# Four later pairs of attention on quarter arrays, one q copy on ScalarE, one multiplication on GpSimd

## The chip, the cores and the metric

The kernel runs on one core of one Trainium2 chip. The metric is the time of one execution on the device in microseconds; the median of three executions of the kernel before is 878.07 us (877.82 to 878.16). Engines are called as in the profile: PE is TensorE (PEld its weight loads), DVE is VectorE, ACT is ScalarE, POOL is GpSimd, SP is SyncE, and a "q" behind a name means the sequencer of that engine.

## The reference

Attention in chunks of 64 positions, head by head, and then a feed-forward layer with a squared ReLU on all 4608 tokens. All inputs are float32 but the two weights, which reach the kernel as 64-bit numbers (pairs of 32-bit words).

```
q_c, k_c, v_c = (t.reshape(8, 8, 9, 64, 64) for t in (q, k, v))   # batch, head, chunk, position, head_dim
scores = q_c @ k_c.T / 8
attn = exp(scores - max(scores))
attn = attn / (sum(attn) + 1e-9)
x = (attn @ v_c) as [4608 tokens, 512]
h = x @ w_in                       # 512 -> 2048
out = relu(h)**2 @ w_out           # 2048 -> 512
```

## The kernel before

**Tiling.** A pair is 128 tokens (two chunks of 64, all eight heads). There are 36 pairs in nine blocks of four. The code counts pairs from 0: pair u = 0 to 3 (the lead, block 0), u = 4 to 7 (block 1, "pairs five to eight"), and 8 to 35, which the class Quad handles. Per block the feed-forward layer has 16 steps; a step of block b and slice f multiplies x of 512 tokens by 128 columns of w_in (line 525, 12 matmuls of 512 columns into the bank h), squares the ReLU on ACT and DVE (lines 536 to 552), and two steps later multiplies by the 128 rows of w_out (line 562, 12 matmuls into four banks o). Each float32 factor is split into a high part and a low part (gh and gl, xh and xl), hence three matmuls for each product.

**Weights.** The 32 weight slices (16 of w_in, 16 of w_out) are converted on the chip before first use, by `convert_w` (line 138): on ACT two reads of the raw words (lines 148, 149), on DVE clamp, shift, sign and up (lines 154, 160, 166, 173), on ACT the high part (line 178), on DVE the low part (line 187, tiles wi and wo). Staging tiles `a` for this come in ABUFS = 3 buffers, used in turn. Slices are converted in the order i0, i1, o0, i2, o1, i3 and so on, while block 0 already runs; all of it is done when block 0 is.

**Attention of pairs 0 to 7 (class Pair).** q and k of a pair are turned by four PE transposes each (line 411). The turned q is copied into the tile qbd by `keep_q` (line 422) in two copies of 64 partitions, each into its own half of a tile whose other half is zero, so that one matmul can contract over 128 partitions; pairs 0 and 1 copy on DVE, the others on ACT. k is copied by ACT (line 426). `scores` is 16 matmul calls against the zero-padded q, 32 matmuls in the trace (line 434). Then on DVE the maximum (line 441) and the subtraction (line 445), on ACT the exponential (line 450), on DVE the sum (line 454), the addition of 1e-9 (line 457; on POOL for pairs 4 to 7), the reciprocal (line 460) and the multiplication (line 461). The result is turned by PE (line 472), copied by ACT (line 477), and multiplied by v (line 486, again 32 matmuls against a zero-padded tile vbd). ACT and DVE write the result as xh and xl (lines 497, 499). The intermediate results of pairs 4 to 7 go in turn through the two PSUM banks of the tile `both`.

**Quad (pairs 8 to 35).** Here scores and values run on quarters of the array (lines 289 and 333): matmuls with 64 contraction rows and 64 columns, four of them on different quarters, with results in the halves of the two banks of `both`; there is no zero padding.

**Order.** The class Plan writes the order of each engine's instructions by hand: every step is added with an engine, an assumed cost, what it reads and writes, and a rank; a simulated run in assumed times sorts them. On the device each engine takes its instructions strictly in that order and waits where something is not ready. The matmuls of the feed-forward layer keep their order among themselves (line="ffn"). Attention of pairs 4 to 7 ranks with the weight slices among which it is added (one pair for every four slices); the steps of pair 8 and later rank behind all conversions.

Of the kernel before, what the change touches and what calls it, by code (L numbers as in the profile page):

```python
# [10 lines left out]
F32 = mybir.dt.float32  # L11
# [4 lines left out]
ALU = mybir.AluOpType  # L16
AX = mybir.AxisListType
# [3 lines left out]
def kernel(  # L21
# [20 lines left out]
    nc = tc.nc  # L42
    B, H, S, D = q.shape
    NT, DM = out.shape
    DFF = w_in.shape[1] // 2
    P = 128
    CH = 64
    NCH = S // CH
# [6 lines left out]
    EXP_MIN = 2.0 ** -15  # L55
    EXP_MAX = 122879.9921875

    ABUFS = 3
    blocks = [4] * 9
    LAG = 2  # L60
    GBUFS = 2
# [43 lines left out]
    def slot_of(pair):  # L105
        return pair if pair < blocks[0] else pair % 2
# [88 lines left out]
    xt = {}  # L195
# [47 lines left out]
    def load_lead_v(pair):  # L243


        for c in range(2):
            bb, n0 = divmod(2 * pair + c, NCH)
            for h2, r in enumerate(halves):
                s = v[bb, h2:H:2, n0 * CH:(n0 + 1) * CH, :]
                nc.sync.dma_start(  # L250
                    out=vbd[slot_of(pair)][r, :, c, h2, :], in_=s.rearrange("h i d -> i h d")
                )
# [13 lines left out]
    class Quad:  # L266
# [26 lines left out]
        def top(self):  # L293
            self.m = att.tile([P, 2, HH, 1], F32, name=f"m{self.pair}", tag="nm", bufs=2)
            nc.vector.tensor_reduce(self.m, four[:, :, 0], axis=AX.X, op=ALU.max)  # L295

        def less(self):
            self.e = late["pool"].tile([P, HH, 2, CH], F32, name=f"e{self.pair}", tag="e")
            nc.vector.tensor_tensor(  # L299
                self.e.rearrange("p h c j -> p c h j"), four[:, :, 0], self.m.broadcast_to([P, 2, HH, CH]),  # L300
                op=ALU.subtract,
            )
# [10 lines left out]
        def norm(self):  # L313
            nc.vector.tensor_tensor(self.e, self.e, self.z.broadcast_to([P, HH, 2, CH]), op=ALU.mult)  # L314
# [66 lines left out]
    class Pair:  # L381
# [36 lines left out]
        def keep_q(self, s):  # L418
            r = halves[s]

            copy = nc.vector.tensor_copy if self.u < 2 else nc.scalar.copy
            copy(qbd[self.u % 2][r, :, s], self.psq[r])

        def keep_k(self):
# [31 lines left out]
        def small(self):  # L456
            (nc.vector if self.lead else nc.gpsimd).tensor_scalar_add(self.z, self.z, 1e-9)

        def norm(self):
            nc.vector.reciprocal(self.z, self.z)  # L460
            nc.vector.tensor_tensor(
                self.e, self.e, self.z.broadcast_to([P, H, CH]), op=ALU.mult
            )

# [26 lines left out]
        def place(self, part):  # L491
            b = block_of[self.u]
            j = self.u - first_pair[b]
            ps = self.xt.rearrange("p a c i -> p a (c i)")
            xh, xl = (x[:, :, j * P:(j + 1) * P] for x in x_of(b))
            if part == 0:
                nc.scalar.copy(xh, ps)
            else:
                nc.vector.tensor_tensor(xl, ps, xh.bitcast(F32), op=ALU.subtract)


    steps = [(b, f) for b in range(len(blocks)) for f in range(NF)]
# [101 lines left out]
    class Plan:  # L604
# [21 lines left out]
        def add(self, engine, cost, fn, reads=(), writes=(), size=0, line=None, slack=0.0, gate=None, side=0):  # L626


            n = len(self.ops)
            before = set()  # L630
            for t in reads:
                if t in self.writer:
                    before.add(self.writer[t])
            for t in writes:
                before.update(self.readers.get(t, ()))
                if t in self.writer:
                    before.add(self.writer[t])
            for t in writes:
                self.writer[t] = n
                self.readers[t] = set()  # L640
            for t in reads:
                self.readers.setdefault(t, set()).add(n)
            after = set() if gate is None else {gate}
            if line is not None:
                if line in self.last:
                    after.add(self.last[line])
                self.last[line] = n
            before.discard(n)
            if side:
                self.sides[n] = side  # L650
            self.ops.append((engine, cost, fn, before, after, size, self.rank, slack))
            return n
# [84 lines left out]
    def program():  # L737
# [2 lines left out]
        p = Plan()  # L740
        lead = blocks[0]
        add = p.add
        prs = [Pair(u) for u in range(NN)]

        def prepare():
            make_identity(nc, ident)
# [21 lines left out]
                    line="sp" if e == SP else None)  # L768

        def load_values(u):  # L770
            add(SP, 4 * ISSUE, lambda: load_lead_v(u), writes=[("v", slot_of(u))], size=P * DM * 4, line="sp")

        def x_names(pair, part):
            b = block_of[pair]
# [9 lines left out]
        def attention(u):  # L784
            x = prs[u]
            i = u % 2
            if x.lead:
                bq, bk, bs = ("o", 2 * i), ("o", 2 * i + 1), ("h", i)
            else:
                bq, bk, bs = (("at", next(turn_at) % 2) for _ in range(3))  # L790
            if 2 <= u < lead:
                bp, bx = bk, bq
            else:
                bp, bx = (("at", next(turn_at) % 2) for _ in range(2))
            x.banks = {"q": bq, "k": bk, "sc": bs, "pt": bp, "xt": bx}
            r = ["early"]
            wait = 0.0 if x.lead else SLACK
            add(PE, 4 * 0.11, lambda: x.turn(0), [("q", u), "ident"], [bq], slack=wait)
            for s in range(2):
                e = DVE if u < 2 else ACT  # L800
                add(e, ONE, lambda s=s: x.keep_q(s), [bq] + r, [("qbd", i, s)])
            add(PE, 4 * 0.11, lambda: x.turn(1), [("k", u), "ident"], [bk], slack=wait)
            add(ACT, ONE, x.keep_k, [bk] + r, [("raw", "qk"[i])])
            if u in (0, lead - 1):
                filler(x, "sc", bs, [bq, bk])
            add(PE, 1.05, x.scores, [("qbd", i, 0), ("qbd", i, 1), ("raw", "qk"[i])] + r, [bs],
                slack=wait)
            add(DVE, TWO, x.top, [bs], [("m", i)])
            add(DVE, TWO, x.less, [bs, ("m", i)] + r, [("e", i)])
            add(ACT, ONE, x.exps, r, [("e", i)])  # L810
            add(DVE, TWO, x.sums, [("e", i)] + r, [("z", i)])
            add(DVE if x.lead else POOL, 0.2 if x.lead else 0.41, x.small, [], [("z", i)])
            add(DVE, TWO + 0.2, x.norm, [("z", i)] + r, [("e", i)])
            if u in (0, lead - 1):
                filler(x, "pt", bp, [bs])
            add(PE, 4 * 0.11, x.turn_p, [("e", i), "ident"] + r, [bp], slack=wait)
            add(ACT, ONE, x.keep_p, [bp] + r, ["tt"])
            if u in (0, lead - 2, lead - 1):
                filler(x, "xt", bx, [bp])
            add(PE, 1.05, x.values, [("v", slot_of(u)), "tt"] + r, [bx], slack=wait)  # L820
            xh, xl = x_names(u, "h"), x_names(u, "l")
            add(ACT, ONE, lambda: x.place(0), [bx], xh)
            add(DVE, TWO, lambda: x.place(1), [bx] + xh, xl)

        def convert(n):
            words, clamp, shift, sign, up, high, low = convert_w(n)
# [198 lines left out]
```

## Time and profile before

| what | value |
|---|---|
| median of three executions | 878.07 us |
| the profiled execution itself | 878.62 us |
| span in its profile, first to last instruction | 876.8 us |
| outside of the span | 1.82 us |
| PE busy | 868.4 us, 99% |
| DVE busy | 443.3 us, 51% |
| ACT busy | 313.8 us, 36% |
| POOL busy | 8.5 us, 1% |

The rows below come from this one profiled execution. A row of the timeline has the start in us from the start of the span, the duration, the engine, the line, the operation, the tiles written and read, the shape and the number of merged instructions; in brackets stands the idle time of the engine before it and what ended that. Consecutive instructions of one engine overlap a little, so that a step takes less of an engine's order than its own duration: the distance from one start to the next tells what it takes.

### The profile page before, as it was taken

Reading aid. Unit: us, or ns where it says so; the run is one execution under the profiler, and the core shown is the slowest. Engines: PE = TensorE matmul, PEld = TensorE weight load, DVE = VectorE, ACT = ScalarE, POOL = GpSimd, SP = SyncE. Lnnn points to the kernel's source line nnn. Section 1 sums busy time; section 2 is a strip of 40 time slices with the busy share of each in tenths; the row PEclk is TensorE's granted clock in tenths of the full one; section 3 lists DMA queues with packets and bytes.
Section 4 is the critical chain, followed back from the end, with each engine's and each line's share of the span. In section 5 each row is a group of like instructions: output and inputs, shape, how many; then the busy total and the mean of one; then the engine's idle time right before and its main releaser. Section 6 shows DMA issues by size and latency. Waiting matters only on the chain.

```text
span 876.8 us, 15293 instructions
## 1 busy us (share of the span) xinstructions
PE 868.4 (99%) x5950; PEld 709.9 (81%) x5950; DVE 443.3 (51%) x770; ACT 313.8 (36%) x537; POOL 8.5 (1%) x16
## 2 busy tenths in 40 slices
PE   9999999999999999999999999999999999999998
PEld 7777778888888888888888888888888888888886
DVE  5999994333444445444544444445444544423222
ACT  5898874333322222222322232223222322222221
POOL 2000000000000000000000000000000000000000
PEclk9999999999999999999999999999999999999999
DMA  8896523233343223222322242224222241001001
GB/s 189 248 257 185 193 33 95 52 53 54 53 96 53 44 48 93 48 45 47 93 48 46 44 94 48 47 47 96 50 48 46 45 95 23 13 1 49 1 0 49
DMA packets 256856, 62.91 MB, mean 72 GB/s; under 512 B 241808, under 2 KB 250256, under 8 KB 256784
## 3 DMA queue, kind: packets, MB, share of 16 engines
q1 hardware_dynamic: 254528, 61.28, 31.3%
q8 instruction: 47, 0.77, 0.4%
q10 hardware_dynamic: 2256, 0.66, 0.3%
q14 instruction: 25, 0.20, 0.1%
HBM read 45.09 MB, written 9.44 MB: 62 GB/s over the span
## 4 chain that ended last, share of the span: by engine, by line
PE 82%; SPq 3%; issue 3%; DVE 1%; DMA 0%; ACT 0%; POOLq 0%; POOL 0%; DVEq 0%; ACTq 0%
PE h L525 40%; PE o L562 39%; PE both L333 2%; SPq L232 2%; PE both L289 1%; SPq L328 1%; SPq L263 0%; DMA k_raw<-in_k_dram 0%; DVE gl L552 0%; DMA v_raw<-in_v_dram 0%; DVE kt L281 0%; DVE wi L187 0%; DVE z L309 0%; PE both L486 0%; DVE e L314 0%
## 5 line engine op out<-in xcount | busy, mean ns | idle before, releaser
L525 PE MATMUL h<-xh,wi 128*128 128x512 f32 x1152 | 388.2, 394 | 1.4 <-ACT wi L178 1.0
L562 PE MATMUL o<-wo,gh 128*128 128x512 f32 x1152 | 355.9, 390 | 0.0
L525 PEld LDWEIGHTS h<-xh,wi 128*128 128x128 f32 x1152 | 215.7, 188 | 51.1 <-DVE wi L187 2.7
L562 PEld LDWEIGHTS o<-wo,gh 128*128 128x128 f32 x1152 | 215.4, 188 | 44.5
L562 PE MATMUL o<-wo,gl 128*128 128x512 f32 x576 | 224.2, 389 | 0.0
L525 PE MATMUL h<-xl,wi 128*128 128x512 f32 x576 | 223.9, 390 | 0.0
L552 DVE TENSOR_TENSOR gl<-g,gh 128x512 fp32r<-128x512 f32 x144 | 98.3, 683 | 186.5 <-ACT gh L549 186.5
L536 ACT ACTIVATE g<-h 128x512 f32<-128x512 f32 x144 | 85.5, 594 | 229.4 <-PE h L525 215.9
L549 ACT CAST gh<-g 128x512 fp32r<-128x512 f32 x144 | 89.6, 622 | 207.4 <-PE o L562 168.3
L540 DVE TENSOR_TENSOR g<-g 128x512 f32<-128x512 f32 x112 | 76.3, 681 | 169.1 <-ACT g L536 169.1
L562 PEld LDWEIGHTS o<-wo,gl 128*128 128x128 f32 x576 | 108.1, 188 | 22.6
L525 PEld LDWEIGHTS h<-xl,wi 128*128 128x128 f32 x576 | 108.2, 188 | 21.3
L295 DVE TENSOR_REDUCE m<-both 128x8 f32<-128x512 f32 x28 | 19.4, 691 | 39.6 <-ACT xh L345 39.6
L305 ACT ACTIVATE e<-e 128x512 f32<-128x512 f32 x28 | 17.7, 633 | 52.2 <-DVE e L299 52.2
L345 ACT CAST xh<-both 128x512 fp32r<-128x512 f32 x28 | 16.4, 587 | 37.0 <-PE both L289 36.0
L333 PEld LDWEIGHTS both<-p,v_raw 64*64 64x64 f32 x896 | 15.6, 134 | 9.9 <-issue 9.5
L281 DVE STREAM_TRANSPOSE kt<-k_raw 128x512 f32<-128x512 f32 x28 | 19.0, 678 | 8.1 <-DMA v_raw<-in_v_dram 4.2
L542 ACT ACTIVATE g<-g 128x512 f32<-128x512 f32 x32 | 20.2, 632 | 0.6
L318 DVE STREAM_TRANSPOSE et<-e 128x512 f32<-128x512 f32 x28 | 19.9, 712 | 1.0
L281 DVE STREAM_TRANSPOSE qt<-q_raw 128x512 f32<-128x512 f32 x28 | 19.6, 702 | 0.0
L347 DVE TENSOR_TENSOR xl<-both,xh 128x512 fp32r<-128x512 f32 x28 | 19.1, 681 | 0.8 <-ACT xh L345 0.8
L333 PE MATMUL both<-p,v_raw 64*64 64x64 f32 x896 | 19.4, 224 | 0.0
(84 smaller groups left out, 433.6 us busy)
## 6 DMA issues: line engine op xcount, KB each, us to landing
wiraw<-in_moe_w_in_dram SPq DMA_DIRECT2D x16, 512.0 KB, 6.1
woraw<-in_moe_w_out_dram SPq DMA_DIRECT2D x16, 512.0 KB, 6.2
out_dram<-ob SPq DMA_DIRECT2D x32, 256.0 KB, 2.5
q_raw<-in_q_dram SPq DMA_DIRECT2D x224, 32.0 KB, 2.2
k_raw<-in_k_dram SPq DMA_DIRECT2D x224, 32.0 KB, 2.2
v_raw<-in_v_dram SPq DMA_DIRECT2D x224, 32.0 KB, 2.2
p<-et SPq DMA_DIRECT2D x224, 32.0 KB, 1.9
vbd<-in_v_dram SPq DMA_DIRECT2D x32, 64.0 KB, 2.7
```

Source lines behind the costliest of these rows:

```text
L281: nc.vector.transpose(t.rearrange("p h i -> p (h i)"), pairs[self.pair][nm].rearrange("p h a d -> p (h a d)"))
L295: nc.vector.tensor_reduce(self.m, four[:, :, 0], axis=AX.X, op=ALU.max)
L318: nc.vector.transpose(self.et.rearrange("p h c n i -> p (h c n i)"), self.e.rearrange("p h c j -> p (h c j)"))
L333: nc.tensor.matmul(four[to, b, 1, 2 * a + c], self.v[own, c, a, t], self.p[own, 2 * a + t, c].rearrange("p n i -> p (n i)"), start=True, s ...
L347: nc.vector.tensor_tensor(xl, got, xh.bitcast(F32), op=ALU.subtract)
L525: nc.tensor.matmul(self.h[:, :self.n], a[:, c], bb[:, c, :self.n], start=c == 0 and i == 0, stop=last,)
L536: nc.scalar.activation(self.g, self.h[:, :self.n], AF.Relu)
L540: nc.vector.tensor_tensor(self.g, self.g, self.g, op=ALU.mult)
L542: nc.scalar.activation(self.g, self.g, AF.Square)
L549: nc.scalar.copy(self.gh[:, :self.n], self.g)
L552: nc.vector.tensor_tensor(self.gl[:, :self.n], self.g, self.gh.bitcast(F32)[:, :self.n], op=ALU.subtract)
L562: nc.tensor.matmul(acc[b, j], a[:, j * P:(j + 1) * P], bb, start=f == 0 and i == 0, stop=f == NF - 1 and i == 2,)
```

## The change

Five edits go together. Pairs 4 to 7 become a new class Later, which runs scores and values on quarters of the array, as Quad does: 16 calls each with 64 contraction rows, 32 matmuls in a trace, results in halves of both banks of `both`; q is kept without zero padding in one copy of 128 partitions on ACT; v is loaded by two DMAs in place of four. The two banks of `both` are then held in a fixed way (q and the turned probabilities in the first, k in the second, scores and values in halves of both). For these four pairs the multiplication of the probabilities by the reciprocal moves from DVE to POOL; the reciprocal itself stays on DVE as a step of its own (`part`). In the lead, q of pair 1 is copied by ACT and no longer by DVE. The staging tiles `a` get a fourth buffer. The plan's assumed costs follow: 0.6 in place of 1.05 us for scores and values, 1.1 us for the multiplication on POOL.

```diff
-    ABUFS = 3
+    ABUFS = 4
...
-            copy = nc.vector.tensor_copy if self.u < 2 else nc.scalar.copy
+            copy = nc.scalar.copy if self.u else nc.vector.tensor_copy
...
+        def part(self):
+            nc.vector.reciprocal(self.z, self.z)
+
         def norm(self):
-            nc.vector.reciprocal(self.z, self.z)
-            nc.vector.tensor_tensor(
+            (nc.vector if self.lead else nc.gpsimd).tensor_tensor(
...
+    class Later(Pair):
+        def half(self, n):
+            return four[:, :, n]
+        def load_values(self):
+            self.v = vbd[slot_of(self.u)][:, :HH // 2].rearrange("p a b c d -> p (a b c) d")
+            for c, r in enumerate(halves):
+                bb, n0 = divmod(2 * self.u + c, NCH)
+                s = v[bb, :, n0 * CH:(n0 + 1) * CH, :]
+                nc.sync.dma_start(out=self.v[r], in_=s.rearrange("h i d -> i h d"))
+        def keep_q(self):
+            self.qt = qbd[self.u % 2][:, :HS]
+            nc.scalar.copy(self.qt.rearrange("p h c i -> p (h c) i"), self.psq)
+        def scores(self):
+            out = self.half(0)
+            kt = self.kt.rearrange("p (h c) j -> p h c j", c=2)
+            for g, c, s, w in itertools.product(range(2), repeat=4):
+                own, to = halves[s], halves[w]
+                nc.tensor.matmul(
+                    out[to, s, 2 * g + c], self.qt[own, 2 * g + w, c], kt[own, 2 * g + w, c], start=True, stop=True
+                )
+        def top(self):
+            self.m = att.tile([P, H, 1], F32, name=f"nm{self.u}", tag="nm", bufs=2)
+            nc.vector.tensor_reduce(
+                self.m.rearrange("p (s h) a -> p s h a", s=2), self.half(0), axis=AX.X, op=ALU.max
+            )
+        def less(self):
+            self.e = nat.tile([P, H, CH], F32, name=f"ne{self.u}", tag=f"ne{self.u % 2}")
+            nc.vector.tensor_tensor(
+                self.e.rearrange("p (s h) j -> p s h j", s=2), self.half(0),
+                self.m.rearrange("p (s h) a -> p s h a", s=2).broadcast_to([P, 2, HH, CH]), op=ALU.subtract,
+            )
+        def turn_p(self):
+            self.pt = self.room("pt")
+            for a in range(HH):
+                nc.tensor.transpose(
+                    self.pt[:, a // 2, a % 2].rearrange("p s i -> p (s i)"),
+                    self.e[:, 2 * a:2 * a + 2].rearrange("p c j -> p (c j)"), ident,
+                )
+        def values(self):
+            out = self.half(1)
+            for a, w, c in itertools.product(range(HH), range(2), range(2)):
+                own, to = halves[c], halves[w]
+                nc.tensor.matmul(
+                    out[to, c, a], self.v[own, 2 * a + w], self.t[own, a // 2, a % 2, w], start=True, stop=True
+                )
+        def place(self, part):
+            b = block_of[self.u]
+            j = self.u - first_pair[b]
+            xh, xl = (
+                x[:, :, j * P:(j + 1) * P].rearrange("p h (c i) -> p c h i", c=2) for x in x_of(b)
+            )
+            if part == 0:
+                nc.scalar.copy(xh, self.half(1))
+            else:
+                nc.vector.tensor_tensor(xl, self.half(1), xh.bitcast(F32), op=ALU.subtract)
...
-        prs = [Pair(u) for u in range(NN)]
+        prs = [(Pair if u < lead else Later)(u) for u in range(NN)]
...
+            fn = (lambda: load_lead_v(u)) if u < lead else prs[u].load_values
+            add(SP, (4 if u < lead else 2) * ISSUE, fn, writes=[("v", slot_of(u))], size=P * DM * 4, line="sp")
...
-                bq, bk, bs = (("at", next(turn_at) % 2) for _ in range(3))
-            if 2 <= u < lead:
+                bq, bk = bs, bx = [("at", n) for n in range(2)]
+            if not x.lead:
+                bp = bq
+            elif u >= 2:
                 bp, bx = bk, bq
             else:
                 bp, bx = (("at", next(turn_at) % 2) for _ in range(2))
             x.banks = {"q": bq, "k": bk, "sc": bs, "pt": bp, "xt": bx}
             r = ["early"]
+            both_at = [("at", n) for n in range(2)]
+            sc, xt = ([bs], [bx]) if x.lead else (both_at, both_at)
             wait = 0.0 if x.lead else SLACK
             add(PE, 4 * 0.11, lambda: x.turn(0), [("q", u), "ident"], [bq], slack=wait)
-            for s in range(2):
-                e = DVE if u < 2 else ACT
-                add(e, ONE, lambda s=s: x.keep_q(s), [bq] + r, [("qbd", i, s)])
+            if x.lead:
+                for s in range(2):
+                    e = ACT if u else DVE
+                    add(e, ONE, lambda s=s: x.keep_q(s), [bq] + r, [("qbd", i, s)])
+            else:
+                add(ACT, ONE, x.keep_q, [bq] + r, [("qbd", i, 0), ("qbd", i, 1)])
             add(PE, 4 * 0.11, lambda: x.turn(1), [("k", u), "ident"], [bk], slack=wait)
             add(ACT, ONE, x.keep_k, [bk] + r, [("raw", "qk"[i])])
             if u in (0, lead - 1):
                 filler(x, "sc", bs, [bq, bk])
-            add(PE, 1.05, x.scores, [("qbd", i, 0), ("qbd", i, 1), ("raw", "qk"[i])] + r, [bs],
+            add(PE, 1.05 if x.lead else 0.6, x.scores, [("qbd", i, 0), ("qbd", i, 1), ("raw", "qk"[i])] + r, sc,
                 slack=wait)
-            add(DVE, TWO, x.top, [bs], [("m", i)])
-            add(DVE, TWO, x.less, [bs, ("m", i)] + r, [("e", i)])
+            add(DVE, TWO, x.top, sc, [("m", i)])
+            add(DVE, TWO, x.less, sc + [("m", i)] + r, [("e", i)])
             add(ACT, ONE, x.exps, r, [("e", i)])
             add(DVE, TWO, x.sums, [("e", i)] + r, [("z", i)])
             add(DVE if x.lead else POOL, 0.2 if x.lead else 0.41, x.small, [], [("z", i)])
-            add(DVE, TWO + 0.2, x.norm, [("z", i)] + r, [("e", i)])
+            add(DVE, 0.2, x.part, [], [("z", i)])
+            add(DVE if x.lead else POOL, TWO if x.lead else 1.1, x.norm, [("z", i)] + r, [("e", i)])
             if u in (0, lead - 1):
                 filler(x, "pt", bp, [bs])
             add(PE, 4 * 0.11, x.turn_p, [("e", i), "ident"] + r, [bp], slack=wait)
             add(ACT, ONE, x.keep_p, [bp] + r, ["tt"])
             if u in (0, lead - 2, lead - 1):
                 filler(x, "xt", bx, [bp])
-            add(PE, 1.05, x.values, [("v", slot_of(u)), "tt"] + r, [bx], slack=wait)
+            add(PE, 1.05 if x.lead else 0.6, x.values, [("v", slot_of(u)), "tt"] + r, xt, slack=wait)
             xh, xl = x_names(u, "h"), x_names(u, "l")
-            add(ACT, ONE, lambda: x.place(0), [bx], xh)
-            add(DVE, TWO, lambda: x.place(1), [bx] + xh, xl)
+            add(ACT, ONE, lambda: x.place(0), xt, xh)
+            add(DVE, TWO, lambda: x.place(1), xt + xh, xl)
 
         def convert(n):
             words, clamp, shift, sign, up, high, low = convert_w(n)
```

## Rows read from the trace of the kernel before

**Rows 1.** The page: the span, busy time of each engine with its share of the span and its instructions, and the busy tenths of PE and DVE in 40 slices of 21.9 us.

```profile
span 876.8 us, 15293 instructions
...
PE 868.4 (99%) x5950; PEld 709.9 (81%) x5950; DVE 443.3 (51%) x770; ACT 313.8 (36%) x537; POOL 8.5 (1%) x16
...
PE   9999999999999999999999999999999999999998
...
DVE  5999994333444445444544444445444544423222
```

**Rows 2.** Busy time of each engine (and instructions) in three stretches: the stage in which block 0 runs and weights are converted, the end of the conversions, and the rest. Behind it PE's granted clock, the DMA share and GB/s.

```profile
30.70:130.00 99.30, 97.23 (x678) 76.09 (x679) 97.05 (x187) 86.66 (x156) 2.42 (x4) 1.00 0.60 175
130.00:148.00 18.00, 18.00 (x81) 14.88 (x80) 10.92 (x19) 8.05 (x15) 0.00 (x0) 1.00 0.26 50
148.00:876.80 728.80, 725.00 (x4796) 595.43 (x4794) 313.64 (x523) 201.73 (x338) 0.00 (x0) 1.00 0.26 52
```

**Rows 3.** Timeline of DVE and PE around three low parts of w_in (line 187) and the next matmul that needs one (line 525): steps 12, 13 and 15 of block 0.

```profile
109.19 0.69 DVE L187 TENSOR_TENSOR wi<-wia,wi 128x512 fp32r<-128x512 f32 x1
...
109.93 0.73 PE L525 MATMUL h<-xh,wi 128*128 128x512 f32 x2
...
116.28 0.69 DVE L187 TENSOR_TENSOR wi<-wia,wi 128x512 fp32r<-128x512 f32 x1
...
117.03 0.50 PE L525 MATMUL h<-xh,wi 128*128 128x512 f32 x1
...
128.25 0.69 DVE L187 TENSOR_TENSOR wi<-wia,wi 128x512 fp32r<-128x512 f32 x1
...
128.99 0.73 PE L525 MATMUL h<-xh,wi 128*128 128x512 f32 x2
```

**Rows 4.** Waits of DVE between 30.7 and 130 us (us in total, times, longest), and the group of the multiplication of pairs 4 to 7 in the groups by line of the same stretch (busy us, mean ns, idle before).

```profile
DVE gl L552 <- ACT gh L549: 0.8, 2, 0.5
...
L461 DVE TENSOR_TENSOR ne<-ne,nz 128x512 f32<-128x512 f32 x4 | 2.8, 692 | 0.1
```

**Rows 5.** Timeline of DVE and POOL around the multiplication of pair 4.

```profile
51.78 0.68 DVE L173 CUSTOM_DVE_ANT_0 woa<-woraw,woa 128x1024 uint16<-128x1024 uint16 x1
...
51.96 0.60 POOL L457 TENSOR_SCALAR nz<-nz 128x8 f32<-128x8 f32 x1 [45.31 <-DVE nz L454]
...
52.59 0.20 DVE L460 RECIPROCAL nz<-nz 128x8 f32<-128x8 f32 x1
...
52.83 0.69 DVE L461 TENSOR_TENSOR ne<-ne,nz 128x512 f32<-128x512 f32 x1
...
53.44 0.69 DVE L552 TENSOR_TENSOR gl<-g,gh 128x512 fp32r<-128x512 f32 x1
```

**Rows 6.** Timeline of DVE and ACT in the last part of the conversions: a staging tile's last reader on DVE, the next slice's first reads on ACT, and two transposes of pair 8 between steps of conversions on DVE.

```profile
119.63 0.69 DVE L187 TENSOR_TENSOR wo<-woa,wo 128x512 fp32r<-128x512 f32 x1
...
120.77 0.66 ACT L148 ACTIVATE wia<-wiraw 128x512 f32<-128x512 f32 x1
...
121.77 0.71 DVE L281 STREAM_TRANSPOSE qt<-q_raw 128x512 f32<-128x512 f32 x1
...
122.40 0.65 DVE L173 CUSTOM_DVE_ANT_0 woa<-woraw,woa 128x1024 uint16<-128x1024 uint16 x1
...
123.30 0.71 DVE L281 STREAM_TRANSPOSE kt<-k_raw 128x512 f32<-128x512 f32 x1
...
123.93 0.39 DVE L160 TENSOR_SCALAR wia<-wia 128x512 uint32<-128x512 uint32 x1
```

**Rows 7.** Timeline of the lead from 9.8 to 13.8 us: q copies, subtraction, exponential, sum, scores and k copies of pairs 0 to 2.

```profile
9.81 0.68 DVE L422 COPY qbd<-q 64x512 f32<-64x512 f32 x1
...
10.42 0.67 DVE L445 TENSOR_TENSOR ne<-sc,nm 128x512 f32<-128x512 f32 x1
...
11.12 0.69 DVE L422 COPY qbd<-q 64x512 f32<-64x512 f32 x1
11.12 0.63 ACT L450 ACTIVATE ne<-ne 128x512 f32<-128x512 f32 x1 [0.36 <-DVE ne L445]
...
11.87 1.15 PE L434 MATMUL sc<-kt,qbd 128*64 128x64 f32 x30 [0.16 <-DVE qbd L422]
...
13.69 0.59 ACT L426 COPY kt<-k 128x512 f32<-128x512 f32 x1 [0.88 <-PE k L411]
13.73 0.69 DVE L441 TENSOR_REDUCE nm<-sc 128x8 f32<-128x512 f32 x1
```

**Rows 8.** Timeline of PE around scores of pair 5 (line 434, zero padded) and of pair 8 (line 289, on quarters): the last matmul of the feed-forward layer ahead of the 32 matmuls and the first one behind them.

```profile
62.71 0.39 PE L562 MATMUL o<-wo,gl 128*128 128x512 f32 x1
...
64.11 0.73 PE L562 MATMUL o<-wo,gh 128*128 128x512 f32 x2
...
123.96 0.39 PE L525 MATMUL h<-xh,wi 128*128 128x512 f32 x1
...
124.90 0.50 PE L525 MATMUL h<-xh,wi 128*128 128x512 f32 x1
```

**Rows 9.** Groups of POOL by line and shape over the whole span: three of them.

```profile
L755 POOL MEMSET vbd<- 128x1024 f32 x4 | 3.6, 952 | 0.0
L457 POOL TENSOR_SCALAR nz<-nz 128x8 f32<-128x8 f32 x4 | 2.4, 605 | 98.6 <-DVE nz L454 98.6
...
masks.py:199 POOL TENSOR_SCALAR_AFFINE_SELECT ident<-ident 128x128 f32<-128x128 f32 x1 | 0.3, 293 | 0.1
```

More of the change, by code (lines that the diff above doesn't have):

```diff
@@ L770, in load_values @@
         def load_values(u):
-            add(SP, 4 * ISSUE, lambda: load_lead_v(u), writes=[("v", slot_of(u))], size=P * DM * 4, line="sp")
+            fn = (lambda: load_lead_v(u)) if u < lead else prs[u].load_values
+            add(SP, (4 if u < lead else 2) * ISSUE, fn, writes=[("v", slot_of(u))], size=P * DM * 4, line="sp")
         def x_names(pair, part):
```

## The prediction

> **What bounds the kernel now.** I read the page first: PE is busy for 868.4 of 876.8 us, DVE for half of the span only, but in the slices from 22 to 130 us DVE stands at nine tenths or more [rows 1]. So I cut the span where the conversions end. From 148 us to the end PE is busy for 725.0 of 728.8 us and DVE for 43% [rows 2]: whatever makes block 0 end earlier moves all of that forward as it stands, and nothing in the change makes that part shorter. From 30.7 to 130 us PE is busy for 97.23 and DVE for 97.05 of 99.30 us [rows 2]. Two engines are full there, and the question is which one the other waits for. The timeline tells: the low parts of slices i12, i13 and i15 leave DVE at 109.88, 116.97 and 128.94 us (start plus duration), and the matmul that needs each one starts at 109.93, 117.03 and 128.99 us, 0.05 to 0.06 us later, behind gaps that a running PE doesn't have [rows 3]. PE is idle for 2.07 us in that stage [rows 2] and DVE waits for ACT for 0.8 us [rows 4]. DVE with its conversions sets the pace, PE is close behind, and the last such slice (128.94 us) is the point from which PE runs alone to the end. The sum below is therefore the sum of what DVE does ahead of that point.
>
> **The change, part by part.**
>
> *The multiplication leaves DVE.* Four instructions of 0.69 us [rows 4]. In DVE's order one takes less, since neighbours overlap: from 52.83 to the next start at 53.44 it is 0.61 us [rows 5]. 4 x 0.61 = 2.44 us, all ahead of 128.94 us. The reciprocal and the addition stay as they are. Pair 4's probabilities are ready later than now if POOL is slower than DVE, and only PE's transpose (line 472), the copy behind it and the values wait for that; feed-forward matmuls queued behind the transpose would wait too, which PE's idle time and the part after next can cover.
>
> *What the multiplication costs on POOL, and what it does to DVE.* No row shows it. For 512 columns the nearest rows give 0.48 us (half of a memset of 1024 columns, 0.952 us) to 1.17 us (four times a select of 128 columns, 0.293 us) [rows 9], estimates from one stream and from another operation. In DVE's time the bounds are nothing and the whole of it, 1.17 us for each pair, if DVE stands still while POOL works. The nearest row of both engines at once is the addition on POOL: it runs from 51.96 to 52.56 us beside a DVE step that starts at 51.78 us and takes its ordinary 0.68 us [rows 5]. DVE isn't slowed there, so I take nothing; but the row speaks of 8 columns, and it has a second face: 0.605 us for 8 columns where 128 took 0.293 [rows 9], ending 0.10 us after the DVE step did [rows 5], looks like POOL waiting for DVE. If one waits for the other this way round, the other way round is possible, and that is the main rival.
>
> *Scores and values on quarters.* From the last feed-forward matmul ahead of scores to the first one behind it is 1.40 us now (62.71 to 64.11) and 0.94 us on quarters (123.96 to 124.90) [rows 8]: 0.46 us less, eight times, 3.7 us of PE. As PE waits for DVE, I count nothing for it: it turns into longer waits for the slices. It is the cover under which DVE's gain counts in full, for without it PE (2.07 us idle) could give back little more than 2 us. One q copy of 128 partitions in place of two of 64 takes 0.6 us from ACT for each pair, which isn't the bound either (86.66 of 99.30 us) [rows 2]. Two DMAs fewer for v: SP's queue only gets shorter. A pair now holds both banks until xl is written, so the next pair's q turns later than now; that is hidden as long as pair 7 ends before block 1 needs it, behind 128.99 us, and costs PE its place in line if it isn't.
>
> *The fourth staging tile.* Late in the stage DVE does two transposes of pair 8, which rank behind every conversion, at 121.77 and 123.30 us, 0.63 us each to the next start [rows 6]: conversions weren't ready. The first reads of the last slice by ACT start at 120.77 us, 0.45 us after the low part at 119.63 us has left DVE at 120.32 us [rows 6], as a staging tile is freed. With a fourth tile such a read can go earlier and the transposes later. Bounds: 0 and 1.26 us. I take 0.4, nearer to nothing, for the transposes may be needed at that time by an order that I can't see.
>
> *q of pair 1 on ACT.* Two copies leave DVE, 0.6 us each in its order (9.81 to 10.42 us is one) [rows 7], 1.2 us at most. But ACT must then do two q copies, a k copy and the exponential of pair 0 between 9.81 us, when DVE's first copy starts now, and the scores: at 0.59 to 0.63 us each about 2.4 us, so that scores of pair 1 start near 12.2 us where they did at 11.87; with 1.15 us of scores, pair 1's maximum could then start near 13.4 to 13.5 us where it did at 13.73 [rows 7]. ACT has 0.88 us of waiting ahead of the next k copy [rows 7] to catch up. I take a gain of 0.3 us, bounds -0.6 (ACT's chain decides) and +1.2.
>
> *Sum.* 2.44 + 0 + 0 + 0.4 + 0.3 = 3.1 us: the profiled execution would go from 878.62 us (span 876.8 and 1.82 around it) to 875.5 us, and the median, 0.55 us below it, from 878.07 to 875.0 us. With the bounds of start and staging the forecast's own range is 2.44 - 0.6 = 1.8 to 2.44 + 1.2 + 1.26 = 4.9 us, 873.2 to 876.2 us. If PE were the bound after all, the sum would be 3.7 + 0.3 = 4.0 us, 874.1 us, inside of that.
>
> **The rivals.**
>
> *DVE stands still while POOL multiplies.* For: the ending of POOL's addition behind DVE's step [rows 5], and that the DVE steps ahead of and behind the multiplication read two SBUF tiles each [rows 5]. Against: the unchanged 0.68 us [rows 5]. With a hold of 0.48 to 1.17 us (mean 0.83) a pair gives 0.61 and takes 0.83: 4 x 0.22 = 0.9 us lost, less 0.7 from start and staging, 878.3 us (876.9 to 879.6): no change. The Trainium skill has this as a rule: by "SBUF — State Buffer", section "Who interferes with whom", a DVE instruction with two SBUF inputs and a GpSimd instruction that reads SBUF share one port under an exclusive lock, and the second one waits for the first to finish. The traces so far bear out at most POOL's half of it. The skill's page "GPSIMD Engine Reference", section 3.1, gives 4497 ns for two inputs of 2048 columns; a quarter of it, 1.12 us as an estimate, would make the sum 4 x 0.51 - 0.7 = 1.3 us slower, 879.4 us. No row here shows such an instruction.
>
> *The same hold, longer: slower.* POOL's multiplication reads two tiles and may first wait for the DVE step ahead of it. If DVE is held for 0.60 + 1.17 = 1.77 us a pair, DVE loses 4 x (1.77 - 0.61) = 4.6 us, less 0.7: +3.9 us, 882.0 us. It decides from a hold of 0.61 + (1.76 + 0.7)/4 = 1.23 us on, just above the upper bound from the rows; hence a small chance.
>
> *The freed DVE time isn't used.* If ACT's chain delays the lead by 0.6 us and conversions wait for ACT where they now wait for DVE, half of the 2.44 us stays: 0.6 us faster, 877.5 us, no change. For: ACT is at 87% of the stage [rows 2]. Against: it loses 0.6 us a pair, and it is DVE that has next to no waits [rows 4].
>
> *More than the forecast.* PE's 3.7 us and DVE's gain reach beyond 4.9 us only if the order of conversions also improves: some 872 us.
>
> **How the numbers follow.** Forecast 0.50, more than it 0.05, DVE held 0.25, time not used 0.10, held longer 0.10. About 0.2%, 1.76 us, is what a measurement of this kernel can tell from no change: faster means below 876.3, slower above 879.8 us. Faster: 0.50 + 0.05 = 0.55; same: 0.25 + 0.10 = 0.35; slower 0.10. The predicted time is the forecast's, 875.0 us. The range reaches from the forecast's low end, rounded to 873.0, to the end of the first rival, 879.6 us; it leaves out the 0.05 and the 0.10.
>
> **What the profile will show.** Right: the low part of i15 leaves DVE near 125.8 us in place of 128.94; PE still meets the slices within 0.1 us of their end, with more idle time than 2.07 us ahead of that point; groups of 32 matmuls on quarters at 0.94 us; POOL at 0.5 to 1.2 us a multiplication; DVE steps beside POOL at 0.42 and 0.69 us. Wrong: DVE steps of 1 us and more, or gaps in DVE, beside the four POOL instructions (held); the first feed-forward matmul later than 30.70 us (lead); gaps of PE ahead of line 472 (POOL late); no slice met at its end any more (PE the bound). The forecast fails above all if POOL's multiplication takes more from DVE than the 0.61 us that it gives.

## The result

The changed kernel takes 886.0 us (median of 5, 885.1 to 886.91) against 878.07 us (877.82 to 878.34): 1.0089 times as long, 95% interval 1.0075 to 1.0103. It was forecast 3.1 us faster and is 7.9 us slower. The profiled execution has a span of 883.4 us, 6.6 us more than before [rows 1].

The page of the changed kernel, then its busy times by stretch (PE, PEld, DVE, ACT, POOL, each with its instructions, then granted clock, DMA share, GB/s). Line numbers have moved: 525 is now 596, 562 is 633, 536 to 552 are 607 to 623, 461 is 463.

```profile
span 883.4 us, 15266 instructions
...
PE 866.0 (98%) x5950; PEld 707.2 (80%) x5950; DVE 442.3 (50%) x764; ACT 312.4 (35%) x535; POOL 13.8 (2%) x20
...
PE   9899999999989999999999999999999999999998
...
DVE  5999994333544445444444444445444544423222
```

```profile
30.70:130.00 99.30, 93.73 (x654) 72.92 (x652) 97.49 (x184) 83.87 (x151) 7.74 (x8) 1.00 0.57 173
130.00:148.00 18.00, 18.00 (x109) 14.66 (x109) 10.79 (x19) 7.80 (x14) 0.00 (x0) 1.00 0.33 60
148.00:883.00 735.00, 726.73 (x4796) 596.38 (x4794) 313.70 (x523) 201.67 (x338) 0.00 (x0) 1.00 0.26 51
```

Beside [rows 2] two things stand out. From 30.7 to 130 us PE is idle for 5.6 us in place of 2.07, while DVE is as full as before: PE is busy for 3.5 us less, and all of that has become waiting, most of it for w_in slices from DVE (4.5 us in six waits, 0.2 us in one before). And behind 148 us, where nothing was to change, PE is idle for 8.3 us in place of 3.8; the page's PE row shows it as an 8 in the twelfth slice (243 to 265 us). To place the loss I followed one matmul through both traces: the first of block 1 starts at 139.56 us before and at 139.52 us after. Block 0 with all its conversions is worth nothing, neither way; the whole loss lies behind it.

**Block 0.** The low part of the last w_in slice leaves DVE at 127.34 us (126.66 plus 0.68) in place of 128.94 [rows 3]. So DVE is 1.6 us earlier there, not 3.1, and that gain is not passed on: from the end of this slice PE runs for 12.18 us without a pause until block 1, in place of 10.62 us. Pair 8 is part of the reason: its two transposes on DVE come at 128.20 and 130.60 us, behind the last w_in slice and no longer ahead of it [rows 6], and so its scores on PE come at 131.95 us in place of 124.28. The next rows are DVE and POOL in the timeline around the multiplication of pair 4, as [rows 5] were.

```profile
53.31 0.64 DVE L187 TENSOR_TENSOR wo<-woa,wo 128x512 fp32r<-128x512 f32 x1
53.57 1.28 POOL L463 TENSOR_TENSOR ne<-ne,nz 128x512 f32<-128x512 f32 x1 [0.42 <-DVE nz L460]
53.87 1.27 DVE L160 TENSOR_SCALAR wia<-wia 128x512 uint32<-128x512 uint32 x1
55.06 0.41 DVE L154 TENSOR_SCALAR woa<-woa 128x512 f32<-128x512 f32 x1
...
108.49 1.30 POOL L463 TENSOR_TENSOR ne<-ne,nz 128x512 f32<-128x512 f32 x1 [0.41 <-PE o L633]
108.92 1.42 DVE L173 CUSTOM_DVE_ANT_0 woa<-woraw,woa 128x1024 uint16<-128x1024 uint16 x1
```

The clamp and shift steps take 0.42 us where no multiplication on POOL runs; the one that starts beside POOL's multiplication takes 1.27 us and ends 0.29 us after POOL. The same happens beside each of the four multiplications, once each: 1.27, 1.26, 1.27 and, in the last two rows, 1.42 us for a step that takes 0.68 us otherwise. That is 3.3 us of DVE held, where 2.44 us were freed.

**Behind block 0.** The timeline of SP's queue (start, time of issue, number of DMAs): first three rows of the kernel before, then the changed kernel between 226 and 254 us; behind them DVE, ACT and PE of the changed kernel between 255 and 261 us:

```profile
225.32 5.24 SPq L263 DMA_DIRECT2D v_raw<-in_v_dram  x8
...
244.40 3.23 SPq L232 DMA_DIRECT2D k_raw<-in_k_dram  x4
247.73 5.23 SPq L263 DMA_DIRECT2D v_raw<-in_v_dram  x8
```

```profile
226.28 10.47 SPq L263 DMA_DIRECT2D v_raw<-in_v_dram  x16
236.85 5.22 SPq L328 DMA_DIRECT2D p<-et  x8
242.11 4.21 SPq L232 DMA_DIRECT2D q_raw<-in_q_dram  x8
246.43 2.72 SPq L651 DMA_DIRECT2D out_dram<-ob  x4
249.20 3.98 SPq L232 DMA_DIRECT2D k_raw<-in_k_dram  x8
```

```profile
255.40 0.71 DVE L281 STREAM_TRANSPOSE kt<-k_raw 128x512 f32<-128x512 f32 x1 [5.62 <-DMA v_raw<-in_v_dram]
...
257.04 0.64 DVE L611 TENSOR_TENSOR g<-g 128x512 f32<-128x512 f32 x1
...
257.77 0.62 ACT L620 CAST gh<-g 128x512 fp32r<-128x512 f32 x1 [7.75 <-DVE g L611]
...
259.69 0.60 ACT L607 ACTIVATE g<-h 128x512 f32<-128x512 f32 x1 [1.31 <-DVE gl L623]
...
260.35 0.50 PE L596 MATMUL h<-xh,wi 128*128 128x512 f32 x1 [3.62 <-ACT g L607]
```

Read it from the bottom up. PE waits 3.62 us for the bank h, which ACT has not read; ACT waits for DVE's square of the step before; that square stands in DVE's order behind the transpose of a pair's k, and the transpose waits 5.62 us for data. The releaser is put down as v, which is issued later; the k DMAs are issued until 253.18 us (247.63 us in the kernel before), and k is what the transpose reads. k is late because 16 v DMAs, two pairs' worth, went through SP's queue at one stretch for 10.47 us, 5.2 us more than one pair's. A smaller wait of PE for ACT (1.31 us) ends at 210.23 us.

The wait costs more than itself. Busy times and clock of the next stretches, then PE's timeline:

```profile
256.30:260.30 4.00, 0.42 (x2) 0.00 (x0) 3.20 (x7) 1.21 (x2) 0.00 (x0) 1.00 0.25 52
260.30:264.00 3.70, 3.65 (x11) 2.87 (x12) 1.38 (x2) 0.62 (x1) 0.00 (x0) 0.64 0.33 53
264.00:268.00 4.00, 4.00 (x18) 3.27 (x17) 0.69 (x1) 1.10 (x2) 0.00 (x0) 0.91 0.34 55
```

```profile
261.83 1.05 PE L596 MATMUL h<-xh,wi 128*128 128x512 f32 x2
262.69 0.63 PE L596 MATMUL h<-xl,wi 128*128 128x512 f32 x1
263.12 1.05 PE L596 MATMUL h<-xh,wi 128*128 128x512 f32 x2
```

Behind the idle 3.6 us the granted clock averages 0.64: for most of that stretch PE runs at its lower level, 1.2 GHz, and starts a matmul every 0.43 us (261.83 to 262.69 for two) in place of 0.23, for nine matmuls some 1.8 us more. So the two waits and the low clock are about 1.3 + 3.6 + 1.8 = 6.7 us of PE's time, and the span is 6.6 us longer.

### The profile page after: what moved, and what is told of

Same layout as the page of the kernel before. It is cut to its first block, busy times and chain, and to the rows that moved or that the text cites. A ratio compares the mean times of both kernels' runs of the same rounds, so it can differ in the third digit from the quotient of the medians.

```text
span 883.4 us, 15266 instructions
## 1 busy us (share of the span) xinstructions
PE 866.0 (98%) x5950; PEld 707.2 (80%) x5950; DVE 442.3 (50%) x764; ACT 312.4 (35%) x535; POOL 13.8 (2%) x20
## 4 chain that ended last, share of the span: by engine, by line
PE 85%; DVE 9%; issue 2%; SPq 2%; ACT 1%; DMA 0%; POOL 0%; DVEq 0%; POOLq 0%; ACTq 0%
PE h L596 40%; PE o L633 40%; PE both L333 2%; PE both L289 1%; SPq L232 1%; DVE wia L173 1%; DVE wia L166 1%; DVE woa L166 1%; DVE wi L187 1%; DVE woa L173 1%; DVE gl L623 1%; DVE wia L160 1%; SPq L328 1%; DVE woa L154 1%; PE both L823 1%
```

## The experiments

Two questions: which of the five edits puts v ahead of k behind block 0, and why block 0 gains nothing. Theory S: the fourth staging tile does the first. The v tiles of pairs 8 to 35 come from the same staging tiles as the conversions (line 257), so that a fourth one lets v of a further pair be loaded at once, while q and k still wait for their single tiles. Theory P: DVE stands still for most of each multiplication on POOL. The last column is the start of block 1's first matmul in each profile (139.56 us before, 139.52 us after); three more sets of executions of the kernel before, each beside one set of runs, have medians of 878.58, 878.14 and 878.42 us, so that medians of different sets compare to some 0.5 us.

| run | quarter arrays | multiplication on | q of pair 1 on | staging tiles | v | median (range), us | block 1 from, us |
|---|---|---|---|---|---|---|---|
| before | no | DVE | DVE | 3 | free | 878.07 | 139.56 |
| after | yes | POOL | ACT | 4 | free | 886.0 | 139.52 |
| a3 | yes | POOL | ACT | 3 | free | 881.48 (880.73 to 881.99) | 141.55 |
| b4 | no | DVE | DVE | 4 | free | 885.1 (884.35 to 887.76) | 141.47 |
| v3 | yes | POOL | ACT | 4, v in 3 | free | 879.81 (877.78 to 881.06) | 140.34 |
| dn | yes | DVE | ACT | 4 | free | 883.16 (881.85 to 884.27) | 137.72 |
| a4k | yes | POOL | ACT | 4 | behind k | 878.15 (877.45 to 878.76) | 139.15 |
| dnk | yes | DVE | ACT | 4 | behind k | 875.5 (875.2 to 875.77) | 137.01 |
| dnkq | yes | DVE | DVE | 4 | behind k | 876.95 (874.66 to 877.21) | 137.98 |
| hold2k | yes | POOL, twice | ACT | 4 | behind k | 885.02 (883.06 to 885.3) | 146.69 |
| b4k | no | DVE | DVE | 4 | behind k | 880.07 (879.86 to 880.7) | 142.13 |
| bk | no | DVE | DVE | 3 | behind k | 878.07 (877.33 to 878.77) | 140.15 |
| d3k | yes | DVE | ACT | 3 | behind k | 877.75 (876.52 to 877.92) | 139.30 |
| dnkw4 | yes | DVE | ACT | 4 | behind k | 876.5 (875.05 to 877.84) | 136.34 |

**a3, b4 and v3: the staging tiles.** In the changed kernel (a3) and, alone, in the kernel before (b4):

```diff
-    ABUFS = 4
+    ABUFS = 3
```

```diff
-    ABUFS = 3
+    ABUFS = 4
```

and in v3 only the tags and names of the v tiles (three places):

```diff
-        t = wst.tile([P, 2, HH // 2, 2, D], F32, name=f"v_raw{pair}", tag=f"a{pair % ABUFS}")
+        t = wst.tile([P, 2, HH // 2, 2, D], F32, name=f"v_raw{pair}", tag=f"a{pair % 3}")
```

> The changed kernel with three staging tiles as before, all else as changed. Theory S (the fourth staging tile lets v of a later pair be loaded early, ahead of k on SP's queue, and DVE and PE then wait for k): the idle time of PE behind block 0 (1.3 and 3.6 us) goes, 878 us within 1. Rival H (VectorE held by GpSimd's multiplication delays block 0, and all else follows from that): still 884 us or more. Rival Q (the new use of the two banks and the later start of each pair shifts the order of loads): still 884 us or more.

> The kernel before with four staging tiles and nothing else. Theory S: slower by 4 to 7 us, 882 to 885 us, with PE idle in blocks 2 and 3 behind a transpose of k on DVE. Rivals H and Q: no change or a little faster, 876.5 to 878.5 us.

> The changed kernel; the conversions keep four staging tiles, the v tiles of pairs 8 to 35 go through the first three of them only, as before. Theory S: 877 to 879 us, no idle time of PE behind block 0. Rivals H and Q: 884 us or more.

b4 is decisive: one number changed in the kernel before, ratio 1.0082 (1.0066 to 1.0097), with 16 v DMAs in a row from 227.14 us and a wait of PE of 4.2 us behind them. Not all of its 7 us is that loss: 1.9 us of them lie in block 0, which b4k below shows too. v3 takes most of the changed kernel's loss back (ratio 1.0014, 1.0005 to 1.0023) and keeps one wait of 1.4 us. a3 missed its number by over 2 us (ratio 1.0036, 1.0023 to 1.0049): the waits behind block 0 shrink to two of 1.3 us together, as S expects, but with three tiles and POOL's multiplication block 0 itself ends 2 us later. Some 1.6 of these 2 us are the clock: behind a wait of 1.62 us for a w_in slice the granted clock is 0.88 between 110 and 120 us (1.00 in the changed kernel), and matmuls start 0.43 us apart until 120.5 us. H and Q expected 884 us or more of a3 and v3 and no loss of b4: they fall as causes of the loss behind block 0.

**a4k: the order on SP's queue alone.** Four tiles stay; v is put in line behind the same pair's k.

```diff
-            add(SP, 8 * ISSUE, x.load_values, [], [("a", pair % ABUFS)], size=P * DM * 4)
+            add(SP, 8 * ISSUE, x.load_values, [], [("a", pair % ABUFS)], size=P * DM * 4, line=("raw", "k"))
```

> The changed kernel with one edit in the plan: the load of a pair's v stands in line behind the same pair's k loads (pairs 8 to 35), with four staging tiles for all. Theory S (v loaded ahead of k on SP's queue makes DVE and PE wait behind block 0): PE no longer waits behind block 0, and block 0 ends where it ends in the changed kernel, 877 to 879 us. Rival C (it is the number of staging tiles itself, by another way than the order on SP's queue): 884 us or more.

886.0 becomes 878.15 us; against the kernel before 1.0 (0.9991 to 1.0009). SP's queue in its timeline; one pair's v at a time, and k issued by 240.5 us in place of 253.2:

```profile
228.12 5.23 SPq L328 DMA_DIRECT2D p<-et  x8
233.40 1.09 SPq L232 DMA_DIRECT2D q_raw<-in_q_dram  x2
234.53 2.93 SPq L232 DMA_DIRECT2D k_raw<-in_k_dram  x6
237.56 1.87 SPq L651 DMA_DIRECT2D out_dram<-ob  x4
239.48 1.03 SPq L232 DMA_DIRECT2D k_raw<-in_k_dram  x2
240.55 6.08 SPq L263 DMA_DIRECT2D v_raw<-in_v_dram  x8
```

No transpose on DVE waits for a DMA between 200 and 300 us here (5.6 and 4.1 us of such waits in the changed kernel). That settles S, and rival C falls: what costs the 7.85 us is the order, not the number of tiles. In bk the same line in the kernel before changes nothing.

> The kernel before with v behind k on SP's queue and nothing else. It tells whether the order of loads alone helps the kernel before, which has no waits behind block 0: within 0.5 us of 878.1 us.

**dn and dnk: the multiplication back on DVE.** dn with v free, dnk with v behind k; in both:

```diff
-            (nc.vector if self.lead else nc.gpsimd).tensor_tensor(
+            nc.vector.tensor_tensor(
...
-            add(DVE if x.lead else POOL, TWO if x.lead else 1.1, x.norm, [("z", i)] + r, [("e", i)])
+            add(DVE, TWO, x.norm, [("z", i)] + r, [("e", i)])
```

> The changed kernel with the multiplication of pairs 4 to 7 back on DVE; four staging tiles for all. Theory S: the loss behind block 0 stays (881 to 885 us), block 0 ends within 1 us of where it ends now, since DVE gives back the 0.24 us a pair that being held costs net. Rival H: 876 to 878.5 us.

> As the run before with the multiplication of pairs 4 to 7 back on DVE. Theory P (DVE stands still for most of a multiplication on GpSimd, so that moving it costs more than it frees): block 0 ends 1.5 to 2 us earlier than with it on GpSimd, 875.5 to 877.5 us. Rival F (as forecast, DVE's order is shorter with the multiplication on GpSimd): 1 to 2.5 us later than the run before.

dn keeps the loss behind block 0 (waits of 5.8 us) and ends block 0 1.8 us earlier than the changed kernel, more than the 1 us expected. dnk is the best version: 875.5 us, ratio 0.997 (0.9959 to 0.9982), 2.65 us faster than a4k, which differs from it by the multiplication alone; block 0 ends 2.1 us earlier, a little more than P's 1.5 to 2. F falls. The price is higher than the 0.85 us by which the held time exceeds the freed: PE's waits in block 0 are 5.5 us in sum in a4k and 3.0 us in dnk, and why 0.85 us of DVE moves these waits by 2.5 us was not taken apart. DVE around pair 4's multiplication in dnk, with ordinary durations:

```profile
53.28 0.64 DVE L187 TENSOR_TENSOR wo<-woa,wo 128x512 fp32r<-128x512 f32 x1
53.84 0.68 DVE L463 TENSOR_TENSOR ne<-ne,nz 128x512 f32<-128x512 f32 x1
54.44 0.42 DVE L160 TENSOR_SCALAR wia<-wia 128x512 uint32<-128x512 uint32 x1
```

**hold2k: the suspected cost twice.** To a4k a second multiplication on POOL is added; its result is read by nobody, so that only its effect on DVE and on POOL's next work is left.

```diff
+            if not self.lead:
+                again = att.tile([P, H, CH], F32, name=f"again{self.u}", tag="again")
+                nc.gpsimd.tensor_tensor(again, self.e, self.z.broadcast_to([P, H, CH]), op=ALU.mult)
```

> The changed kernel with v behind k, and GpSimd does the multiplication of pairs 4 to 7 a second time into a tile that nobody reads; nothing waits for the second one but the next pair's. Theory P: a second DVE step beside it takes about 0.85 us longer for each pair (or two steps together do), 3.4 us of DVE in all; block 0 ends 2 to 4 us later than without it, 880 to 882 us. Rival F: DVE steps keep 0.42 and 0.69 us, within 1 us of the run without it.

```profile
54.27 1.28 POOL L463 TENSOR_TENSOR ne<-ne,nz 128x512 f32<-128x512 f32 x1 [0.42 <-DVE nz L460]
54.57 1.27 DVE L160 TENSOR_SCALAR wia<-wia 128x512 uint32<-128x512 uint32 x1
55.63 1.10 POOL L468 TENSOR_TENSOR again<-ne,nz 128x512 f32<-128x512 f32 x1
55.76 1.26 DVE L154 TENSOR_SCALAR woa<-woa 128x512 f32<-128x512 f32 x1
```

Each multiplication holds one DVE step, now two a pair: eight long steps with 6.5 us over their ordinary durations, 3.3 of them new. That is what P expects to 0.1 us. The time moved by more than expected: 6.9 us over a4k, block 1 later by 7.5. Part of that is the clock, as the rows of these two stretches show (the third number from the end is the granted clock; a4k has 1.00 in both):

```profile
60.00:70.00 10.00, 8.91 (x65) 7.10 (x66) 7.78 (x15) 6.99 (x14) 0.00 (x0) 0.83 0.95 286
120.00:130.00 10.00, 7.98 (x28) 6.12 (x28) 9.43 (x19) 7.12 (x13) 0.00 (x0) 0.83 0.00 0
```

In each, behind waits of 1.09 and 2.02 us for a w_in slice, nine matmuls, started 0.43 in place of 0.23 us apart for the most part, take 1.7 us more. So of the 7.5 us about 3.4 are the low clock, 3.0 are longer waits of PE (8.5 in place of 5.5 us in sum), and 1.05 us were there when the feed-forward layer began (31.50 in place of 30.45 us), ahead of every multiplication on POOL.

**dnkq, b4k and d3k: what the other edits are worth.** Each undoes a part of dnk: the q copy back on DVE (dnkq); the whole class Later and the q copy (b4k, made from the kernel before); the fourth tile (d3k).

```diff
-            copy = nc.scalar.copy if self.u else nc.vector.tensor_copy
+            copy = nc.vector.tensor_copy if self.u < 2 else nc.scalar.copy
...
-                    e = ACT if u else DVE
+                    e = DVE if u < 2 else ACT
```

> As the run before with q of pair 1 copied by DVE again, as in the kernel before. If the copy on ACT was worth the 0.3 us of the forecast: 0.3 us slower than the run before; if ACT's chain decides in the lead, up to 0.6 us faster.

> The kernel before with four staging tiles and v of pairs 8 to 35 behind k on SP's queue; no quarter arrays, multiplication on DVE, q of pair 1 on DVE. Against the run with quarter arrays, multiplication on DVE and v behind k (875.5 us). Theory D of the forecast (DVE sets the pace in block 0, PE's 3.7 us of quarter arrays count for nothing): 875 to 876.5 us. Rival E (PE's own work in block 0 counts too): 3 to 4 us slower than that run, 878.5 to 879.5 us.

> Quarter arrays, multiplication on DVE, q of pair 1 on ACT, v behind k, but three staging tiles. If the fourth tile is worth the 0.4 us of the forecast, 875.9 us; if it is worth nothing or DVE's order with three tiles is the better one, 875 us or less; if ACT has to wait for staging tiles more, 877 us or more.

dnkq's median is 1.45 us above dnk's, but what the copy is worth is not settled, nor its sign: two of its eleven executions take 874.7 us, less than any of dnk (875.2 to 875.77), at a granted clock of 0.999; the nine others take 876.5 to 877.2 us at 0.997 to 0.998. In the profiled one (876.5 us) PE waits 2.0 us in block 0 for xl, and the clock is 0.83 between 90 and 100 us, where dnk has 1.00. b4k is 4.6 us slower than dnk and 3.1 us slower than dnkq's median. Theory D expected it at 875 to 876.5 us and is wrong for this run; E's 878.5 to 879.5 is nearer. Where PE waits in block 0, b4k first, then one line of bk, which has three tiles, then dnk (engine, line, what it waited for: us in total, times, longest):

```profile
PE both L411 <- ACT qbd L422: 2.8, 3, 1.1
PE h L525 <- DVE wi L187: 1.0, 3, 0.4
PE h L525 <- ACT wi L178: 0.8, 1, 0.8
```

```profile
PE both L411 <- ACT qbd L422: 0.5, 2, 0.2
```

```profile
PE h L596 <- DVE wi L187: 1.4, 2, 0.8
PE both L411 <- DVE xl L570: 0.7, 1, 0.7
PE both L411 <- ACT qbd L521: 0.7, 1, 0.7
PE h L596 <- ACT wi L178: 0.2, 1, 0.2
```

In b4k PE waits 2.8 us for the second of two q copies before it may turn k, against 0.7 us in dnk. That wait does not belong to the zero-padded pairs as such: in bk, which has them too, it is 0.5 us. It comes with the fourth tile, and it is as large as the 2.0 us by which b4k is slower than bk. So b4k does not tell PE's own work from that wait, and E is not shown by it.

d3k is 2.25 us slower than dnk, and only 0.3 us faster than bk, within the spread of both. Four runs with the multiplication on DVE and v behind k make a square:

| median, us | 3 staging tiles | 4 staging tiles |
|---|---|---|
| zero-padded pairs, q of pair 1 on DVE | 878.07 (bk) | 880.07 (b4k) |
| class Later, q of pair 1 on ACT | 877.75 (d3k) | 875.5 (dnk) |

The class Later with the q copy is worth 0.3 us with three tiles and 4.6 with four; the fourth tile costs 2.0 us without the class and gains 2.25 with it. Neither has a price of its own. How the order brings that about is open.

**dnkw4: w_in ahead of w_out.** In dnk's `convert`:

```diff
             a = ("a", n % ABUFS)
+            if items[n][0] == "o" and n > 3:
+                p.rank += 4
```

> The 875.5 us kernel with the conversion of w_out slices four ranks later, so that a w_in slice often goes ahead of the w_out slice in front of it. Theory D (the w_in slices on DVE set the pace in block 0, while w_out slices are ready 5 to 10 us ahead of their use): waits of PE for w_in slices get shorter, 873 to 875 us. Rival E (PE's own work decides): 875 to 876 us.

Block 0 ends 0.7 us earlier, but PE then waits 1.3 us behind it again, and 1.2 us in block 0 for slices of w_out: 876.5 us, no gain. D's 873 to 875 us fails; E's 875 to 876 us is missed by 0.5.

## Why the prediction was wrong

The medians make a closed chain from the kernel before to the changed one. It is one path of several, and by the square above the second and third links would be other numbers on another path: bk 878.07; fourth tile (b4k) +2.0; class Later on quarter arrays (dnkq) -3.1; q copy on ACT (dnk) -1.45; multiplication on POOL (a4k) +2.65; v no longer held behind k (the changed kernel) +7.85: 886.0 us. By the prediction's own steps:

- *The fourth staging tile*, +0.4 us gained, is the step that failed. It spoke of conversions and took the tile to be theirs alone. The code says otherwise: `load_v` takes the same tiles. A buffer count moves steps on a queue, here v loads ahead of k loads on SP's, and the prediction did not weigh that: of SP's queue it said that it only gets shorter. The price was 7.85 us (a4k), a wait of PE and the low clock behind it, which no rival named. For the conversions the forecast had the movement right: both transposes of pair 8 go behind the last w_in slice in every run with four tiles. Its worth was 2.25 us beside quarter arrays, outside of the 0 to 1.26 us given, and a loss of 2.0 us in the kernel before.
- *What POOL does to DVE*, taken at nothing, was the other failure. The first rival had the mechanism and the hold right: 3.3 us in all, near its 0.83 us a pair, against 2.44 us freed; and the forecast's own sign of being wrong, DVE steps of 1 us and more, came out. The rival's price of 0.9 us was too small: 2.65 us from dnk to a4k. That a4k's 878.15 us is next to the rival's 878.3 is luck, for a4k also has what class and tile give together. The row of the addition on POOL [rows 5] could not show the hold: at 8 columns POOL is done 0.10 us after DVE's step; its odd 0.605 us was the hint. The Trainium skill, "SBUF — State Buffer", section "Who interferes with whom", says that a VectorE instruction with two SBUF inputs contends with a GpSimd instruction that reads SBUF, under an exclusive lock; the trace agrees for the held step that reads two tiles, with 1.42 us for a step of 0.68 us. The estimate of 1.12 us from "GPSIMD Engine Reference", section 3.1, in the Trainium skill stands beside 1.28 us measured.
- *Quarter arrays*, counted at nothing: in the changed kernel block 1 starts when it did, with 3.5 us less of work for PE and 3.5 us more of waiting ahead of it, as forecast; and with three tiles the class and the q copy are worth 0.3 us (d3k against bk). With four tiles and the multiplication on DVE the class is worth some 3 us (dnkq against b4k), of which 2.8 us of waits for q copies in b4k may be the larger part; the 3.7 us of PE work that [rows 8] gave is near it, but not shown to be the cause. The premise that PE waits for DVE was thinner than it looked: in the kernel before PE waits 0.2 us for DVE's w_in slices and 1.0 us for ACT's, and in dnk the last slice ends at 125.50 us and its matmul starts at 125.56 us, yet 0.23 us after the matmul ahead of it, so without a gap. With 2% idle on either engine neither can be called the bound.
- *q of pair 1*: 0.3 us forecast, not settled; the first feed-forward matmul starts between 30.4 and 31.6 us in all runs, with and without it.
- *That what lies behind block 0 moves as it stands* was false as used. The order behind it comes from the same plan, and a buffer count changed it.

The predicted 875.0 us is near dnk's 875.5, but by accident: there the class and the fourth tile give together what the multiplication was to give.

## What to carry to other kernels

Before raising a buffer count, list every user of the buffers: here a transfer that could start earlier went through an in-order queue ahead of transfers that were needed sooner, and the loss appeared where the buffer's first user had long finished. The multiplication moved to GpSimd beside a full VectorE was paid for in VectorE's own steps, 0.82 us for each 0.61 us freed; compare the hold with what is freed, and test it by doing the moved work twice. Where two engines are both nearly full in a hand-written order, don't add up one engine's column: take the edits away one by one and in pairs, for two of them here are worth something only together. And look at the granted clock of a stretch before putting its whole delay down to waits.

## What the runs showed of the hardware

One GpSimd multiplication of 128x512 float32 (1.04 to 1.41 us, mostly 1.28) lengthened exactly one VectorE step each time, by 0.74 to 0.85 us: a clamp or shift of one SBUF tile as much as steps that read two. An idle time of PE of 3.6 us was followed by a granted clock of 0.64 over the next 3.7 us, at a cost of some 1.8 us on top of the wait. Shorter waits went both ways: behind 1.31 us that ended at 210.23 us of the changed kernel the clock stayed at 1.00, and behind 1.09 us that ended at 61.09 us of hold2k, soon after one of 0.36 us, it fell, at a cost of 1.7 us.
